# New orders for groups 1 to 8 of a linear-attention and GELU kernel: three seven-product units in group 2

## The chip, the cores and the metric

The kernel runs on one core of one Trainium2 chip. The metric is the device time of one execution in microseconds (us); the kernel before is given by the median of three runs. One execution was also taken with the hardware profiler.

## The reference

Inputs q, k and v have the shape (8 batches, 8 heads, 576 positions, 64 wide); the weights are `w_in` (512 x 2048) and `w_out` (2048 x 512). For each batch and head:

```
phi(x) = where(x > 0, x, exp(x) - 1) + 1
kv  = phi(k).T @ v                  # 64 x 64
z   = sum of phi(k) over positions  # 64
x   = (phi(q) @ kv) / (phi(q) @ z + 1e-6)
h   = x @ w_in                      # the 8 heads side by side: 512 wide
out = gelu_tanh(h) @ w_out          # 4608 x 512, float32
```

## The kernel before

The work is cut into nine groups, j = 0 to 8. Groups 0 to 7 take the first 512 positions of one batch each; group 8 takes the last 64 positions of all eight batches together. While TensorE (PE in the profile) makes the two large products of group j, the attention of group j + 1 is put between them.

Both large products are made by a scheme of seven products with sums instead of eight products without (Strassen in Winograd's form). For `h`, class `Quad` (L997) takes a unit of 512 columns of `h`, called X, Y, Z or W by its place. One unit is seven products of four matmuls with 256 columns each (L1007), and between them VectorE (DVE) and ScalarE (ACT) copy and add on the accumulator banks. Where there is no unit, a block of 128 columns is made plainly: word `p`, four matmuls with 512 columns (L365), followed by one GELU, word `g`. A unit stands in place of four `p`. The seven products of the second matmul, words `o1` to `o7`, have 16 matmuls with 256 columns each (L812).

The order of all instructions on all engines is written out, one string for each group, `ORDER_A` (group 0) to `ORDER_I` (group 8). `iteration` (L1073) goes through the words of a string, and each engine executes its own instructions in the order of the words. So a word that waits holds up everything behind it on its engine. The words that matter here, with `U` for one of X, Y, Z, W:

| word | what it issues | line |
|---|---|---|
| `U1` ... `U7` | one product of a unit, 4 matmuls | L1007 |
| `Us` | copies `U1` into the seed bank, where `U2` then adds (ACT; DVE with a ') | L1041 |
| `Um`, `Uu` | copies of a bank into SBUF (m: DVE, ACT with a '; u: ACT, DVE with a ') | L1046, L1050 |
| `Uc`, `Ua` | additions on DVE | L1035 |
| `Ug11` ... `Ug22` | the four GELUs of a unit on ACT | L1022 |
| `S1:a-b` ... `S4:a-b` | sums of the GELU results for blocks a to b, on DVE: `S3` before `o7`, `S2` before `o6` | L772 |
| `os`, `oc11`, `oc12`, `oc21`, `oc22`, `om`, `ou` | copies and additions after the `o` products | L902 to L933 |
| `!xs` | four differences of the next group's x on DVE, used by products 7, 6, 5, 4 | L995 |
| `n0` ... `n3` | attention of one chunk: 4 matmuls, then a division on DVE | L287, L304, L305 |
| `k` | phi(k).T @ v, 72 small matmuls, then two DVE copies | L271, L630 |
| `t0`, `t1`, `!qta`, `!qtb`, `!rt` | transposes of x and of phi(q) on TensorE, then a copy (ACT; DVE with a ') | L664, L644, L654 |
| `!ke`, `!qe`, `!re` | exp on ACT | L240 |
| `!kx`, `!qx`, `!rx`, `!km`, `!qm`, `!rm` | the other parts of phi on DVE | L248, L256 |
| `!vc` | cast of v (ACT; DVE with a ') | L260 |
| `!lk`, `!lq`, `!lv`, `!lr` | loads from the SP queue into a pool of seven buffers | L90, L99, L113 |
| `!t` | loads the table of GELU on ACT | L398 |
| `@1` | stores of the group before, issued by ACT | L946 |

There are six single accumulator banks and one pair. The seed bank goes from unit to unit: `Us` of the next unit writes it after `Ug11` of the unit before has read it. exp and GELU are in different tables. Where ACT comes to a function whose table is not there and no `!t` stands ahead, the compiler writes a table load just ahead of that function, behind those waits of it that are written as instructions of their own.

Two of the seven load buffers hold sums for good, and from group 2 on a third holds rows of the units (word `!br`). A load gets the buffer that comes free first, and SP issues its loads in the order of the words.

Of the kernel before, what the change touches and what calls it, by code (L numbers as in the profile page):

```python
# [17 lines left out]
def kernel(  # L18
# [293 lines left out]
    xs = {}  # L312
# [760 lines left out]
    def iteration(j):  # L1073
# [65 lines left out]
        "o0:12-16 @32 o1:12-16 @33 !qe:2 o2:12-16 @34 o3:12-16 @35"  # L1139
    )  # L1140
    ORDER_B = (
        "!qx:2 !qm:2 p8 !ke:2 p5 !t p1 p0 !qtb:2' !kx:2 g0 p2 g1 g2 !vc:2' p3 g3 !km:2 !lk:3 p11 "
        "p4 g4 g5 !a0 p7 p6 g6 !a2 g7 !a3 k2 !lv:3 !qta:2 o1 os' g8 @2 p9 p12 p10 !qx:3 g9 n0 "
        "T0-8 !lk:4 p14 g10 g11 g12 p13 n1 g13 !lq:4 g14 !kxb:3 p15 g15 o7 S1:2-3 S1:1-2 S1:0-1 "
        "!ke:3 o2 S1:3-8 S2:0-8 om !qe:3 n2' !vc:3 t0 n3 o6 !kxa:3 ou' o4 o5 !qm:3 !qtb:3 S4:0-8 "
        "oc22 oc21 t1 !km:3 !qta:3' o3 oc12' !xs oc11'"
    )
    ORDER_C = (
        "k3 p0 p14 Z1 !lv:5 !ke:4 !kx:4 !t p6 Z7 !br Zs g6 @1 Z6 Zu Zm n1 Z2 !qx:4 Zg11 g14 p8 Z5 "
        "Y1 !km:4 Zc g0 g8 Ys Y7 p7 Z4 n2 Y6 Ym' !lv:4 g7 !lk:5 Y2 Yg11 Z3 Zg12 Zg22 p15 Y4 Yu' "  # L1150
        "Za Ya Y5 Yc p1 Zg21 g15 g1 n3' n0 Yg22 Y3 Yg12 o1 Yg21 p9 S1:3-8 S3:4-8 os g9 t1' t0 "
        "S1:0-3 o2 !qe:4 S3:0-4 S2:0-8 o7 om !xs S4:0-8 o6 ou' !qm:4 o4 !vc:4 o5 !kx:5 !ke:5 oc22 "
        "oc11 oc21 !qta:4' k4 o3 oc12' !km:5"
    )
    ORDER_D = (
        "X1 Y1 !lq:5 !t Xs !qtb:4' X2 Xg11 Ys X6 Xu' n0 X7 Z1 Y2 !lk:6 Xm' Yg11 X5 Zs Xc Xg22 Y7 "
        "Ym n1 Y6 Yu' X3 Xg12 Z2 @1 X4 Xa Zg11 W1 Ws Xg21 Y4 Ya Yg21 Y5 Yc Z6 Zu' W6 Wu' Yg22 Z7 "
        "Zm' W2 Y3 Wg11 W7 Wm' Yg12 Z5 !vc:5' W5 Zc Z4 Zg22 Za W4 Wc Wa Z3 Zg12 S1:0-6 Wg22 Zg21 "
        "o1 os W3 Wg12 Wg21 S2:0-6 t0 S1:6-8 k5 S2:6-8 S3:0-8 !qx:5 n2' S4:0-8 o2 !ke:6 o6 !kx:6 "
        "!lv:6 ou o7 om !qe:5 n3 o5 oc11 o4 !vc:6 !qm:5 oc22 oc21 t1' !qta:5' !qtb:5 !xs o3 oc12"  # L1160
    )
    ORDER_E = (
        "X1 Xs !t X7 n2 Xm Y1 X6 !lq:6 X2 Xu' Xg11 n1 Y7 X4 Ys Z1 Ym' Y2 @1 X5 !km:6 Xc Yg11 Zs "
        "Y6 Y4 Xa Yu Ya !lr:0 k6 Xg22 Xg21 Z6 Zu' X3 Yg21 Z2 Zg11 !rx:0 W1 Ws Y5 Yc n3 Z7 Z5 Zm' "
        "Zc W6 Z4 Xg12 Yg22 !lv:7 Y3 Yg12 W7 Zg22 W2 Wg11 Wu' W5 Z3 Zg12 Wm Wc Wg22 W4 Za n0 W3 "
        "Wa Wg12 S1:0-8 !lk:7 S2:0-8 Zg21 o1 os Wg21 t1 t0 o2 !re:0 o6 S3:0-8 o7 ou oc11 !vc:7' "
        "om !qe:6 S4:0-8 !kx:7 o5 !xs !ke:7 oc22 !qx:6 !re:1 o4 oc21 o3 oc12"
    )
    ORDER_F = (
        "!t !qm:6 X1 Xs' X7 Xm' Y7 Ym !qta:6' X2 Xg11 X6 Y4 Xu' Y1 !km:7 Ys X4 !qtb:6 X5 Xa Xg21 "  # L1170
        "Y2 Xc Xg22 Y6 Yu' Z1 Ya k7 Yg11 Y5 Yc X3 Zs Z7 Xg12 Z2 Zg11 Zm n1 W1 Ws Y3 Z6 W6 @1 "
        "!lq:7 !qx:7 Wu' Yg21 W2 Z4 Zu Z5 Zc Yg12 Yg22 S1:0-4 W7 Wm' n0 Wg11 W5 Z3 Zg12 Wc Zg22 "
        "o1 W3 Wg22 !rm:0 Wg12 t0 S1:4-6 S3:0-6 W4 S1:6-8 S3:6-8 !lr:1 S2:0-4 S2:4-8 n2 o7 os "
        "!rx:1 !qe:7 om' !rm:1 o6 ou' Wa Wg21 n3 Za Zg21 o4 o5 t1 o2 !qm:7 oc22 S4:0-8 oc21 oc11' "
        "!qtb:7 !xs o3 oc12'"
    )
    ORDER_G = (
        "X1 !qta:7' Xs X7 Y7 Ym' @1 X2 Xg11 Xm n2 X6 Y1 !rt:0' Ys Y4 n0 Xu Y6 Y2 !rx:2 Z1 X4 Yu "
        "Yg11 Ya Zs X5 Y5 Z2 Z6 Yg21 Xa Xg21 Xc Zu' Zg11 W1 Yc n3 Z7 Ws X3 Xg12 W6 Wu' Xg22 Zm "
        "Yg22 Z5 Y3 W7 Wm' W2 Zc W5 Wc Z4 Yg12 W4 Za Zg22 Wa Wg11 n1 Z3 Zg12 S1:0-6 W3 Wg12 Zg21 "  # L1180
        "Wg22 Wg21 !re:3 o1 os' S1:6-8 S2:0-8 t1' S3:5-8 !rt:1 t0 S3:0-5 S4:0-8 o2 o6 ou o7 oc11 "
        "o5 !re:2 !xs !rm:2 om o4 !rx:3 oc22 o3 oc21 oc12' !t"
    )
    ORDER_H = (
        "X1 Xs n1' n0 X7 Xm' X6 X2 Xu Y1 !rt:2' X5 Xg11 Y7 Z1 Xc Ys Y6 @1 Y2 Yu' Ym' Y4 Ya X4 X3 "
        "Xa Y5 Xg22 Yg11 Zs Z6 Yc Xg12 Yg21 Zu' Z2 Zg11 Xg21 Z7 W1 Y3 Z5 Ws' W7 Yg22 Yg12 W6 Wu "
        "Zm W2 Wg11 Z4 W5 Wm Zc Zg22 !rm:3 Wc Wg22 Z3 Zg12 !rt:3' W4 Wa W3 Wg12 Za Zg21 o1 os "
        "S1:6-8 S1:0-6 S2:0-8 S3:0-8 n3' n2 Wg21 t0' o2 o6 o7 ou o5 om oc22 t1 o4 S4:0-8 oc11 !xs "
        "o3 oc21 oc12'"
    )  # L1190
    ORDER_I = (
        "X1 Xs Y1 X7 X2 Xg11 Xm @1 X6 Ys Xu' X4 Y7 Ym' X5 Y2 Yg11 Z1 Y6 Xa Xg21 Xc Zs' Yu' Y4 Ya "
        "X3 Z6 Z2 W1 Xg22 Xg12 Zg11 Z7 Y5 Zu' Z5 Ws W6 Yg21 Zm W2 Yc Yg22 Wg11 Wu' W7 Y3 Yg12 W5 "
        "Zc Z3 Wm Zg12 Wc Zg22 Z4 Za Wg22 W4 S1:0-6 W3 Wg12 S1:6-8 S2:0-3 S2:3-8 Wa o1 Wg21 "
        "S3:0-8 Zg21 S4:3-8 S4:0-3 o5 o6 o7 o2 o4 o3"
    )
    ORDERS = {0: ORDER_A, 1: ORDER_B, 2: ORDER_C, 3: ORDER_D, 4: ORDER_E, 5: ORDER_F, 6: ORDER_G, 7: ORDER_H, 8: ORDER_I}

# [33 lines left out]
```

## Time and profile before

| | us |
|---|---|
| three runs | 275.84, 276.32 (median), 276.67 |
| the profiled execution | 276.67 |
| its span, first to last instruction | 274.9 |
| around the span | 1.77 |

The profile has one row for a kind of instruction, with busy time, mean duration and the idle time ahead of it. A timeline has one row for consecutive instructions of one kind: start, time taken, engine, line, result and operands, count; the idle time ahead and what ended it stand in square brackets. PEld is the weight load that goes with each matmul and overlaps it; DVE is VectorE, ACT ScalarE, POOL GpSimd. The time recorded for a row of matmuls is some 0.16 us longer than their pitch, because they are pipelined: a product of four takes 0.60 us in its row, and the next begins 0.44 us after its start.

The groups begin at about 48.5 (group 1), 79.5 (2), 108.5 (3), 137 (4), 164 (5), 192.5 (6), 219.8 (7) and 246.7 us (8).

### The profile page before, as it was taken

The numbers are of one execution on the slowest core, as the hardware profiler recorded it, in microseconds if no ns is written. First come the engines' busy times: TensorE is split into PE (matmuls) and PEld (weight loads), VectorE is DVE, ScalarE is ACT, GpSimd is POOL, SyncE is SP. The second block draws the span as 40 slices with busy tenths as digits, with TensorE's granted clock in tenths as the row PEclk, the third lists the DMA queues.
The fourth block names the chain that finished last, engine by engine and source line by source line (L and its number), as shares of the span: only waits on it lengthen the run. The fifth ranks groups of instructions, "written<-read, shape, count | busy, mean of one in ns | idle before, by whom it ended". The sixth has DMA issues, their size and how long they took to land.

```text
span 274.9 us, 7015 instructions
## 1 busy us (share of the span) xinstructions
PE 267.9 (97%) x2988; PEld 215.2 (78%) x2989; DVE 241.1 (88%) x394; ACT 204.7 (74%) x290; POOL 18.4 (7%) x30
## 2 busy tenths in 40 slices
PE   8899999999999999999999999999999999999995
PEld 3484446466977799988989988989999889888884
DVE  2979996898999998999999999999899689967982
ACT  4758876957987797888898898886688388338820
POOL 7057401000000000000000000000000000000000
PEclk9999999999999999999999999999999999999999
DMA  6999999996197019731493055101200030003004
GB/s 229 401 405 397 410 405 401 400 403 244 39 364 238 31 25 346 283 104 55 89 342 147 2 161 148 79 1 41 114 2 0 17 141 0 2 2 154 0 2 153
DMA packets 29327, 46.58 MB, mean 169 GB/s; under 512 B 5232, under 2 KB 15472, under 8 KB 29296
## 3 DMA queue, kind: packets, MB, share of 16 engines
q1 hardware_dynamic: 26416, 37.23, 38.2%
q10 hardware_dynamic: 2880, 8.91, 8.0%
q8 instruction: 23, 0.38, 0.6%
q14 instruction: 8, 0.07, 0.1%
HBM read 36.70 MB, written 9.44 MB: 168 GB/s over the span
## 4 chain that ended last, share of the span: by engine, by line
PE 82%; DVE 6%; DMA 5%; ACT 2%; SPq 2%; POOL 1%; issue 1%
PE o_ps L812 31%; PE hq_ps L1007 25%; PE h_ps L365 6%; DMA w_st<-in_moe_w_in_dram 5%; PE h_ps L812 4%; PE h_ps L1007 4%; PE n_ps L287 2%; PE t_ps L664 2%; PE o_ps L739 2%; PE t_ps L644 2%; PE kv_ps L271 2%; DVE w_B L977 2%; DVE w_near L977 2%; DVE w_A L977 1%; SPq L90 1%; ACT k_e L240 1%
## 5 line engine op out<-in xcount | busy, mean ns | idle before, releaser
L812 PEld LDWEIGHTS <-g 128*128 128x128 f16 x624 | 60.3, 98 | 7.0
L812 PE MATMUL o_ps<-w_out_sb,g 128*128 128x256 f16 x384 | 45.7, 273 | 0.0
L365 PE MATMUL h_ps<-xt,w_in_sb 128*128 128x512 f16 (+2 forms) x212 | 37.8, 327 | 0.2 <-ACT g L385 0.2
L1022 ACT ACTIVATE g<-hq_ps 128x512 f16<-128x512 f32 x52 | 31.1, 620 | 3.4 <-PE hq_ps L1007 1.3
L1007 PEld LDWEIGHTS <-w_in_sb 128*128 128x128 f16 x312 | 30.2, 98 | 4.1
L365 PEld LDWEIGHTS <-w_in_sb 128*128 128x128 f16 x212 | 17.9, 98 | 14.6 <-issue 0.5
L812 PEld LDWEIGHTS <-s 128*128 128x128 f16 x272 | 26.5, 98 | 3.2
L385 ACT ACTIVATE g<-h_ps 128x512 f16<-128x512 f32 x40 | 22.3, 602 | 7.5 <-PE h_ps L365 7.3
L305 DVE TENSOR_TENSOR xs<-n_ps,r 128x512 f16<-128x512 f32 (+1 forms) x42 | 25.3, 603 | 1.4
L1007 PE MATMUL hq_ps<-t_sum,w_near 128*128 128x256 f16 x168 | 24.2, 272 | 0.0
L1007 PEld LDWEIGHTS <-w_near 128*128 128x128 f16 x224 | 21.4, 98 | 2.9
L933 DVE TENSOR_TENSOR o_sb<-o_ps,o_sb 128x512 f32<-128x512 f32 (+1 forms) x21 | 13.0, 636 | 7.6 <-PE o_ps L812 3.9
L1022 ACT ACTIVATE g<-h_ps 128x512 f16<-128x512 f32 x26 | 16.1, 619 | 4.6 <-PE h_ps L1007 4.3
L1035 DVE TENSOR_TENSOR rows<-hq_ps,rows 128x512 f32<-128x512 f32 x26 | 17.8, 686 | 1.0 <-PE hq_ps L1007 0.2
L240 ACT ACTIVATE q_e<-q_x 128x2048 bf16<-128x2048 f32 (+1 forms) x9 | 15.5, 1722 | 3.3 <-DMA q_x<-in_q_dram 3.2
L1035 DVE TENSOR_TENSOR hq_ps<-hq_ps,rows 128x512 f32<-128x512 f32 x26 | 17.5, 693 | 0.5 <-PE hq_ps L1007 0.2
L240 ACT ACTIVATE k_e<-k_x 128x2304 bf16<-128x2304 f32 (+1 forms) x9 | 17.2, 1910 | 0.8 <-DMA k_x<-in_k_dram 0.7
L1022 ACT ACTIVATE g<-rows 128x512 f16<-128x512 f32 x26 | 16.7, 652 | 1.2 <-DVE rows L1035 1.2
L1041 ACT COPY h_ps<-hq_ps 128x512 f32<-128x512 f32 x23 | 13.1, 571 | 5.9 <-PE hq_ps L1007 5.4
L1007 PE MATMUL h_ps<-xt,w_in_sb 128*128 128x256 f16 x104 | 15.6, 272 | 0.0
L812 PE MATMUL o_ps<-w_B,g 128*128 128x256 f16 x128 | 15.3, 273 | 0.0
L812 PE MATMUL o_ps<-w_near,s 128*128 128x256 f16 x128 | 15.3, 273 | 0.0
(129 smaller groups left out, 512.5 us busy)
## 6 DMA issues: line engine op xcount, KB each, us to landing
out_dram<-o_sb ACTq DMA_DIRECT2D x16, 512.0 KB, 3.0
k_x<-in_k_dram SPq DMA_DIRECT2D x7, 1152.0 KB, 10.6
v_x<-in_v_dram SPq DMA_DIRECT2D x7, 1152.0 KB, 9.0
q_x<-in_q_dram SPq DMA_DIRECT2D x6, 1024.0 KB, 7.8
w_st<-in_moe_w_in_dram SPq DMA_DIRECT2D x3, 1024.0 KB, 13.5
q_x<-in_q_dram SPq DMA_DIRECT2D x4, 512.0 KB, 8.9
w_st<-in_moe_w_out_dram SPq DMA_DIRECT2D x2, 1024.0 KB, 10.7
w_st<-in_moe_w_out_dram SPq DMA_DIRECT2D x4, 512.0 KB, 9.1
```

What stands on the lines that cost most here:

```text
L240: nc.scalar.activation(o, i, AF.Exp)
L271: nc.tensor.matmul(kv_of(a, ii)[HP * s : HP * (s + 1)], lhsT=kp[r, j, u, :], rhs=vp[r, j, u, :], start=(j == 0), stop=(j == J - 1), skip_g ...
L305: nc.vector.tensor_tensor(x_v, n_v[heads + (slice(0, D),)], r[heads + (None,)].to_broadcast(shape + [D]), op=ALU.mult,)
L365: nc.tensor.matmul(h_ps[:, ts], lhsT=w_in_sb[:, c, P * m : P * (m + 1)], rhs=xt[:, c, ts], start=(c == 0), stop=(c == KM - 1), skip_group_ ...
L385: nc.scalar.activation(g_v, h_v, AF.Gelu_apprx_tanh)
L812: nc.tensor.matmul(ps[t] if type(ps) is list else ps[:, t, :], lhsT=lhs[:, m, P * t : P * (t + 1)], rhs=rhs[:, m, :], start=(first and m = ...
L933: nc.vector.tensor_tensor(out, i0, i1, op=ALU.add)
L977: nc.vector.tensor_tensor(out, i0, i1, op=op)
L1007: nc.tensor.matmul(ps[:, f], lhsT=lhs[:, c, P * f : P * (f + 1)], rhs=rhs[:, c], start=(first and f == 0 and c == 0), stop=(c == KM // 2 - 1),
L1022: nc.scalar.activation(g_v, src, AF.Gelu_apprx_tanh)
L1035: add = lambda out, i0, i1: nc.vector.tensor_tensor(out, i0, i1, op=ALU.add)
L1041: on(nc.scalar.copy, nc.vector.tensor_copy)(self.seed, self.b)
```

## The change

Only the strings `ORDER_B` to `ORDER_I` are changed. In group 2 the plain blocks `p0`, `p1`, `p8`, `p9` with their four GELUs are replaced by the unit X, so that the group has three units and four plain blocks instead of two and eight. All groups from 1 on are put in a new order: copies move between ACT and DVE (the mark '), sums are cut at other places, and some steps go to another group. Among them: `!ke:4` from group 2 to group 1, `!km:5` and the first transposes of q of batch 4 from 2 to 3, the loads `!lv:5` from 2 to 3, `!lq:6` from 4 to 3, `!lq:7` from 5 to 4 and `!lr:0` from 4 to 2, `!rx:0` from 4 to 3. In group 5 `!qe:7` goes behind the last GELUs; group 6 has its `!t` at the end, as before. Group 0 and the functions stay as they are.

Cut to groups 2, 3 and 6 and one place of 5:

```diff
     ORDER_B = (
...
     ORDER_C = (
-        "k3 p0 p14 Z1 !lv:5 !ke:4 !kx:4 !t p6 Z7 !br Zs g6 @1 Z6 Zu Zm n1 Z2 !qx:4 Zg11 g14 p8 Z5 "
-        "Y1 !km:4 Zc g0 g8 Ys Y7 p7 Z4 n2 Y6 Ym' !lv:4 g7 !lk:5 Y2 Yg11 Z3 Zg12 Zg22 p15 Y4 Yu' "
-        "Za Ya Y5 Yc p1 Zg21 g15 g1 n3' n0 Yg22 Y3 Yg12 o1 Yg21 p9 S1:3-8 S3:4-8 os g9 t1' t0 "
-        "S1:0-3 o2 !qe:4 S3:0-4 S2:0-8 o7 om !xs S4:0-8 o6 ou' !qm:4 o4 !vc:4 o5 !kx:5 !ke:5 oc22 "
-        "oc11 oc21 !qta:4' k4 o3 oc12' !km:5"
+        "Z1 @1 !br Z7 !t p14 p6 Zs' Z2 g6 Zg11 !kx:4 Zm Y1 Z6 p7 g14 !lv:4 !lr:0 Z4 Ys g7 Y7 Y6 "
+        "!km:4 Y2 Ym' Zu' Z5 Yu Za Zg21 Y4 Yg11 p15 Zc Z3 !qx:4 Ya X1 g15 Xs' Zg22 Zg12 k3 Y5 Yc "
+        "Yg21 X6 X7 Xu n1 X2 Xm' Xg11 Yg22 X5 Xc Xg22 n2' X4 Xa n3 Y3 Yg12 X3 Xg12 S1:0-8 S2:0-8 "
+        "Xg21 o1 os !vc:4 t1 n0 !qe:4 o2 S3:0-8 S4:0-8 o6 ou' !lk:5 k4 !kx:5 t0 !xs o7 o5 om o4 "
+        "!ke:5 oc22 oc11 oc21 o3 !qm:4 oc12'"
     )
     ORDER_D = (
-        "X1 Y1 !lq:5 !t Xs !qtb:4' X2 Xg11 Ys X6 Xu' n0 X7 Z1 Y2 !lk:6 Xm' Yg11 X5 Zs Xc Xg22 Y7 "
-        "Ym n1 Y6 Yu' X3 Xg12 Z2 @1 X4 Xa Zg11 W1 Ws Xg21 Y4 Ya Yg21 Y5 Yc Z6 Zu' W6 Wu' Yg22 Z7 "
-        "Zm' W2 Y3 Wg11 W7 Wm' Yg12 Z5 !vc:5' W5 Zc Z4 Zg22 Za W4 Wc Wa Z3 Zg12 S1:0-6 Wg22 Zg21 "
-        "o1 os W3 Wg12 Wg21 S2:0-6 t0 S1:6-8 k5 S2:6-8 S3:0-8 !qx:5 n2' S4:0-8 o2 !ke:6 o6 !kx:6 "
-        "!lv:6 ou o7 om !qe:5 n3 o5 oc11 o4 !vc:6 !qm:5 oc22 oc21 t1' !qta:5' !qtb:5 !xs o3 oc12"
+        "!t !lv:5 X1 !rx:0 !vc:5' !lq:5 Xs !qta:4' Y7 Ym' Y1 X2 Xg11 Y4 X7 !km:5 X6 !qtb:4' Ys Y6 "
+        "Xu X5 Xm' Yu Y2 Yg11 Xc Xg22 Z1 Ya Yg21 Zs' n1 X4 X3 Y5 Yc Xg12 Z2 W1 Zg11 !lv:6 Ws Xa "
+        "Z6 Zu' Y3 Z7 W6 Yg12 Z5 Zm Wu' Zc W7 W2 Yg22 Xg21 Wm' W5 Wc n0 Z3 Zg22 Z4 Wg11 W3 W4 "
+        "Wg22 o1 S1:0-4 S3:0-4 @1 Zg12 Wa Wg12 S1:4-8 Wg21 S3:4-8 Za S2:0-6 S2:6-8 os k5 !vc:6 "
+        "n2' o7 om Zg21 !lk:6 !qe:5 o6 S4:0-8 t0 !lq:6 ou' n3 o2 oc11 o5 t1 !qx:5 !qm:5 oc22 "
+        "!ke:6 !xs o4 o3 oc21 oc12 !kx:6"
     )
...
     ORDER_F = (
...
-        "!lq:7 !qx:7 Wu' Yg21 W2 Z4 Zu Z5 Zc Yg12 Yg22 S1:0-4 W7 Wm' n0 Wg11 W5 Z3 Zg12 Wc Zg22 "
-        "!rx:1 !qe:7 om' !rm:1 o6 ou' Wa Wg21 n3 Za Zg21 o4 o5 t1 o2 !qm:7 oc22 S4:0-8 oc21 oc11' "
+        "Zg22 Wg12 t0 S1:4-6 S1:6-8 S3:4-8 Z4 S2:0-8 Wg21 n3 Za o7 os !qx:7 !rx:1 !rm:1 n2' om "
+        "Zg21 o6 o4 !rm:0 ou o5 S4:0-8 !qe:7 oc22 t1' o2 oc21 o3 oc11 !qm:7 !xs oc12 !qtb:7'"
...
     ORDER_G = (
-        "X1 !qta:7' Xs X7 Y7 Ym' @1 X2 Xg11 Xm n2 X6 Y1 !rt:0' Ys Y4 n0 Xu Y6 Y2 !rx:2 Z1 X4 Yu "
-        "Yg11 Ya Zs X5 Y5 Z2 Z6 Yg21 Xa Xg21 Xc Zu' Zg11 W1 Yc n3 Z7 Ws X3 Xg12 W6 Wu' Xg22 Zm "
-        "Yg22 Z5 Y3 W7 Wm' W2 Zc W5 Wc Z4 Yg12 W4 Za Zg22 Wa Wg11 n1 Z3 Zg12 S1:0-6 W3 Wg12 Zg21 "
-        "Wg22 Wg21 !re:3 o1 os' S1:6-8 S2:0-8 t1' S3:5-8 !rt:1 t0 S3:0-5 S4:0-8 o2 o6 ou o7 oc11 "
-        "o5 !re:2 !xs !rm:2 om o4 !rx:3 oc22 o3 oc21 oc12' !t"
+        "X1 !qta:7' X7 !rt:0' Xs Xm X2 X6 Y1 Xu' n0 Y7 Xg11 X4 Ys Ym Y2 Xa Z1 n2 Yg11 Zs Y6 Yu @1 "
+        "X5 Xg21 Xc Y4 Z2 Zg11 Ya Yg21 Z6 W1 Ws' Zu' X3 Y5 Yc Xg22 n1 W6 Xg12 Wu Z7 Zm Yg22 Z5 W2 "
+        "Wg11 W7 Wm' Zc W5 Wc Z4 Zg22 Y3 Z3 W4 Za Wa Yg12 n3 Zg12 W3 Wg12 Wg22 Zg21 o1 !rx:2 os "
+        "S1:0-8 S2:0-8 !rt:1' S3:0-8 Wg21 !re:3 t0' t1 o2 o6 ou o7 !rx:3 S4:0-8 oc11' !re:2 om' "
+        "!xs o5 oc22 o4 !t oc21 o3 !rm:3 !rt:3' oc12"
     )
...
```

## The prediction

> **What bounds the kernel now.** I read the page first: span, busy times, and the slices.
>
> ```profile
> span 274.9 us, 7015 instructions
> PE 267.9 (97%) x2988; PEld 215.2 (78%) x2989; DVE 241.1 (88%) x394; ACT 204.7 (74%) x290; POOL 18.4 (7%) x30
> PE   8899999999999999999999999999999999999995
> ```
>
> PE is full in every slice but the first two and the last. Next, what PE waited for from 48.5 us on, where the changed groups begin. The answer has one line:
>
> ```profile
> PE h_ps L365 <- ACT g L385: 0.2, 1, 0.2
> ```
>
> Such a list leaves out short waits, so I also took the starts of successive matmuls against their usual pitch. From 48.5 us to the end of the products that finds 0.36 us in group 1 at 53.1, 0.29 us in group 8 around 248 to 252, 0.10 us at 220.9, and the 0.21 us of switching at each `k`. So PE's own work is the time, and a new order can gain at most that work taken away plus some 0.75 us of waits. The third view, busy time by group (us, then PE, PEld, DVE, ACT, POOL; the rows are groups 2, 3, 4, 5 and 6), says how much the helpers have left:
>
> ```profile
> 79.50:108.50 29.00, 29.00 (x385) 23.11 (x385) 27.47 (x47) 24.63 (x31) 0.00 (x0) 1.00 0.51 173
> 108.50:137.00 28.50, 28.50 (x355) 25.80 (x354) 27.69 (x44) 24.27 (x34) 0.00 (x0) 1.00 0.45 140
> 137.00:164.00 27.00, 27.00 (x330) 24.22 (x328) 26.22 (x42) 24.59 (x36) 0.00 (x0) 1.00 0.48 166
> 164.00:192.00 28.00, 28.00 (x350) 25.15 (x349) 27.20 (x47) 22.46 (x32) 0.00 (x0) 1.00 0.19 62
> 192.00:219.50 27.50, 27.50 (x278) 24.94 (x276) 23.57 (x43) 18.94 (x34) 0.00 (x0) 1.00 0.09 36
> ```
>
> DVE is busy for 95 to 97% of groups 2 to 5 and yet never late: the old order fits to a tenth of a microsecond. The granted clock is 1.00 throughout (the column before the DMA share).
>
> **The change part by part.**
>
> **1. The unit X in group 2.** The chain of waits gives both prices: a plain block, and 28 matmuls with 256 columns.
>
> ```profile
> 89.93 0.86 PE h_ps L365 x4
> ...
> 114.83 3.06 PE hq_ps L1007 x28
> ```
>
> Four blocks are 16 matmuls at 216 ns (the pitch), 3.46 us; the unit is 28 at 109 ns, 3.05 us. PE gains 0.40 us. On ACT four GELUs go and four come, and `Xu`, `Xm'` are new (0.48 us each in a row of copies). On DVE `Xs'`, `Xc`, `Xa` are new (0.60 us each in a row, 0.69 alone), 1.8 us. Who pays for them? In the same group `Zs'` and `Zu'` come to DVE, while `Yu`, the copy of `t1` and that of `!qta:4` leave it, and `!km:5` (1.27 us) goes to group 3: about even. Summed so for every word, with one price for each kind, DVE's work changes by -1.2, -0.2, +1.1, +2.4, -2.4, +1.8, +0.3 and -0.1 us in groups 1 to 8. Up to the end of group 5 the sum is level, and the 1.7 us that are left over fall where DVE has 3 to 6 us free. As a sum, DVE does not become the bound; only its order can cost (4, and the second rival). The cover for these words is PE's 28 us in each group; without it they would cost their 1.8 us.
>
> A rule speaks against this part. The Trainium skill, "Perfetto Trace Analysis", section Identifying the Most-Contended Engine, judges TensorE's headroom by the busy time of weight loads, not of matmuls; that is 78% here. Were the loads the bound, the unit's 12 more at 98 ns would cost 1.2 us where I take off 0.40. The trace shows the matmuls one behind the other at their pitch, so I go by the matmuls.
>
> **2. The table load at the start of group 6.** In group 5 `!qe:7` now comes after the last GELU, and there is no `!t` before `Xg11` of group 6. So the load of GELU's table moves there. The trace of before has one such load, in group 5, and what stands around it matters:
>
> ```profile
> 186.09 1.28 ACT L1022 ACT_TABLE_LOAD   x1 [0.92 <-DVE hq_ps L1035]
> 187.38 1.08 ACT L1022 ACTIVATE g<-hq_ps 128x512 f16<-128x512 f32 x2
> ```
>
> ACT stood idle for 0.92 us until DVE had made the input of the GELU, and only then loaded the table: such a load sits behind the wait of its GELU, not ahead of it. Nothing on PE was near it then. In group 6 PE is: `Xg11` waits for `X2`, `Ys` behind it on ACT needs the seed bank that `Xg11` reads, and `Y2` needs `Ys`. These rows give the steps (PE to copy, copy, GELU to copy):
>
> ```profile
> 192.51 0.60 PE L1007 MATMUL hq_ps<-xt,w_in_sb 128*128 128x256 f16 x4
> 193.14 0.57 ACT L1041 COPY h_ps<-hq_ps 128x512 f32<-128x512 f32 x1 [0.81 <-PE hq_ps L1007]
> ...
> 195.00 0.60 ACT L1022 ACTIVATE g<-h_ps 128x512 f16<-128x512 f32 x1
> ```
>
> From the start of `X2`: its end 0.60, to ACT 0.03, load 1.28, step 0.01, GELU 0.60, step 0.03, copy 0.57, to PE 0.06: `Y2` can start at 3.18 us. By PE's own pitch it would start after `X2`, `X6`, `Y1`, `Y7`, `X4` (0.437 each) and `n0` (0.236): 2.42 us. PE waits 0.76 us. Queued behind it is all of PE; on ACT, `Ys` and all after it. The other end of this cost is nothing, if the load should run ahead of the wait while ACT is idle after `Xs`. I take 0.76, by the row of the one load of this kind. Group 5 keeps its exp table load and loses this one, which held nothing up.
>
> The Trainium skill, "ScalarE: Activation LUTs", section What ACT_TABLE_LOAD costs, adds a drain of about 1.38 us to the load and puts a switch at 2.66 us. By that, an estimate, PE would wait 2.1 us here and the kernel would take 278.4. In the rows above the GELU begins 0.01 us after the load, with no drain between, so I keep 1.28.
>
> **3. `o1` to `o2` in group 2.** `o2` adds to the seed bank that `os` fills with `o1`. Group 4 of before shows the shortest such passage (the matmuls end 0.16 us after the next row's start):
>
> ```profile
> 152.67 1.06 PE L664 MATMUL t_ps<-ident_x,xs 128*128 128x128 f16 x16
> 152.93 0.57 ACT L902 COPY h_ps<-o_ps 128x512 f32<-128x512 f32 x1 [0.72 <-PE o_ps L812]
> ...
> 153.56 0.49 PE L812 MATMUL h_ps<-w_out_sb,g 128*128 128x256 f16 x3
> ```
>
> From the end of `o1` in PE's order (152.67) to `o2` it is 0.89 us, with `o2` starting 0.06 us after the copy ends: all of it needed, and filled there by 16 transposes. The new group 2 has only `t1` (0.445) and `n0` (0.236) between: 0.68. PE waits 0.21 us; at the other end nothing, if `t1` itself is held by the division of `n3` and so fills the gap. I take 0.21.
>
> **4. Sums at the turn from `h` to `out`.** In the new group 3, with 0 at the start of `o1`, `o7` starts at 2.78 (`o1` 1.75, `k` 0.80, `n2` 0.24) and `o6` at 4.53. DVE has `Wc` and the division of `n0` done at -0.3 (`W5` ends at -2.0), then `S1:0-4`, `S3:0-4`, `Wa`, `S1:4-8` at 0.60 each, `S3:4-8` at 0.69: 2.79, just enough. Then `Za` 0.60 and the two pieces of `S2`, 0.87 and 0.42: 4.6, with the step to PE 0.15 too late. I take 0.15; the ends are nothing and 0.4, should DVE enter this stretch late by a copy or two. In group 1, `S1` must wait for `o7` to have read the tile that it writes, and the same count gives `S2` 0.1 to 0.2 after `o6` could start. Against it stand the 0.36 us that group 1 waited at 53.1, which the new order of blocks may shorten; I set both against each other, at nothing, with ends of -0.5 and +0.3.
>
> **5. All else moved.** The number of transposes, attention pieces, exps and explicit table loads is the same over the kernel, so PE's sum changes by part 1 alone. `n0'` instead of `n2'` and the like only exchange one pair of banks for two. Stores at `@1` follow the last copy of the group before on ACT, as they did. The SP queue has the same loads in a new order: `!lr:0` now ahead of `!lk:5`, and `!lv:5` behind it. What hides a load is that its buffer comes free 10 us or more ahead of the use; the tightest is batch 5's v, the third rival. POOL has no work after 45 us. Groups 4, 5, 7 and 8 go at nothing, covered by the same 28 us of PE; their ends are -0.3 (the waits in group 8) and +0.3 each.
>
> **The sum.** -0.40 + 0.76 + 0.21 + 0.15 = +0.72 us. The profiled execution took 276.67 us, a span of 274.9 and 1.77 around it; it would become 277.4. It stands 0.35 above the median of 276.32, so for the median I predict 277.0, or 0.26% more: just inside the 0.3% (0.83 us) that a measurement of this kernel can tell from no change.
>
> **The rivals.**
>
> *The load runs early, the order fits.* ACT loads the table after `Xs` while it waits, or the wait is covered. Then -0.40 + 0.36 at most is left, or -0.7 with group 1's wait gone: 275.6 to 276.3, say 276.0. For it: the old order had no such slips. Against: the row at 186.09.
>
> *DVE is late at every turn.* Place: `S1` to `S3` in groups 1 to 5, where DVE is busy for 95% and more. Price: if it reaches each turn 0.2 to 0.3 us late, +1.0 to +1.5 on top of the sum less its own 0.15, so 278.1 (277.4 to 279). It decides the verdict from 0.1 us in all. For it: group 4's DVE work grows by 2.4 us. Against: level sums to the end of group 5.
>
> *Batch 5's v lands late.* The cast `!vc:5'` is DVE's second step in group 3, and the load can only be issued when a buffer is free. If that is batch 4's v, cast 2.7 us after the end of `o1` in group 2, there are 10.7 us until `!vc:5'`.
>
> ```profile
> v_x<-in_v_dram SPq DMA_DIRECT2D x7, 1152.0 KB, 9.0
> ```
>
> 9.0 us fit. If the buffer is that of batch 5's k, free only 1.8 us before group 3, DVE stands for 6 us, and everything behind it; PE goes on for some 2 us until copies and banks are missing: +4, so 281.
>
> **How the numbers follow.** My forecast, 277.0 (276.6 to 277.5), has 0.46; the early load 0.18; DVE at every turn 0.27; the late v 0.05; a new order that also clears all old waits, under 275.5, 0.04. Of the forecast four tenths lie above 277.15, so slower has 0.18 + 0.27 + 0.05 = 0.50, the same 0.28 + 0.18 = 0.46, faster 0.04. The range goes from 275.8 (inside the early load's case) to 278.8 (inside DVE's); about 2 in 10 is left out.
>
> **What would show it.** Part 1: in group 2, 28 more matmuls at L1007 and 16 fewer at L365. Part 2: early in group 6 a table load at L1022 with idle time ahead of it that `X2` ended, and a hole of some 0.76 us in PE before a product into h_ps. Part 3: 0.2 us between `n0` and `o2` in group 2. Part 4: waits of PEld at L812 for DVE at L772. Wrong would be a load in group 6 right behind `Xs`, or PE waiting in group 3 for banks behind the cast at L260.

## The result, and the profile after

The changed kernel takes 277.85 us in the median of four runs (277.71 to 278.00), the kernel before 276.40 beside it on the same chip: 1.0055 times as long, with an interval of 1.0038 to 1.0072. That is 1.45 us more, where 0.7 was forecast. The profiled execution took 277.71 us. From the page of the changed kernel:

```profile
span 275.9 us, 7052 instructions
PE 268.9 (97%) x3000; PEld 216.4 (78%) x3001; DVE 242.4 (88%) x394; ACT 203.4 (74%) x292; POOL 18.9 (7%) x30
PE   8999999999999999999999999999999999999995
```

In slices of 7 us nothing is to be seen: PE looks as full as before. The waits of PE, from 45 us on, show one line more than before:

```profile
PE h_ps L1007 <- ACT h_ps L1041: 0.6, 1, 0.6
PE h_ps L365 <- ACT g L385: 0.2, 1, 0.2
```

The third view is again the busy time by group (us, then PE, PEld, DVE, ACT, POOL), groups 2 to 6 of the changed kernel:

```profile
78.93:107.43 28.50, 28.47 (x390) 23.79 (x388) 26.95 (x44) 24.75 (x34) 0.00 (x0) 1.00 0.54 171
107.43:135.75 28.32, 28.26 (x346) 25.03 (x344) 27.23 (x47) 24.52 (x34) 0.00 (x0) 1.00 0.54 182
135.75:164.18 28.43, 28.32 (x347) 25.12 (x345) 27.34 (x44) 23.78 (x36) 0.00 (x0) 1.00 0.31 107
164.18:192.16 27.98, 27.98 (x346) 25.18 (x344) 26.96 (x46) 21.09 (x33) 0.00 (x0) 1.00 0.29 97
192.16:220.59 28.43, 27.79 (x283) 25.09 (x280) 25.30 (x45) 19.57 (x31) 0.00 (x0) 1.00 0.06 25
```

PE's busy time falls short of the group's length by 0.64 us in group 6 and by up to 0.11 in others. The recorded time of a product overhangs its pitch by 0.16 us, so shorter waits stay hidden in this view. I therefore set the starts of successive matmuls against their pitch, as in the prediction, for both traces. From the first matmul of group 1 to the end of the last matmul it is 222.91 us before (48.53 to 271.44) and 224.37 after (48.10 to 272.47): 1.46 more, as the medians say. The two profiled times lie only 1.04 apart because group 0, which is the same in both, ended 0.43 earlier in the second. The 1.46 us come from these places:

| place (time after) | before | after | what ended the wait | forecast |
|---|---|---|---|---|
| group 2: unit X for four blocks | | -0.40 | 28 x 109 ns for 16 x 216 ns | -0.40 |
| group 2: `o2` (95.4) | 0 | 0.19 | seed copy `os`, ACT | 0.21 |
| group 3: `W2` to `W5` (118.5) | 0 | 0.22 | copy `Wu'`, DVE | 0 |
| group 3: `o6` (125.7) | 0 | 0.06 | sums `S2`, DVE | 0.15 |
| group 4: `X2` (137.4) | 0 | 0.27 | seed copy `Xs`, ACT | 0 |
| group 4: `n0` (148.8) | 0 | 0.16 | division of `n3`, DVE | 0 |
| group 6: `Y2` (196.5) | 0 | 0.81 | seed copy `Ys`, ACT, behind a table load | 0.76 |
| group 7: one more switch to small matmuls | | 0.22 | | 0 |
| group 7: 220.9, gone | 0.10 | 0 | | 0 |
| group 1: 53.1, 52.7 after | 0.36 | 0.36 | a GELU, ACT | 0 |

Together +1.43; the rest is below 0.05 us at any one place. Group 6 in the timeline of the changed kernel:

```profile
194.15 0.60 PE L1007 MATMUL h_ps<-xt,w_in_sb 128*128 128x256 f16 x4
...
194.83 1.28 ACT L1022 ACT_TABLE_LOAD   x1 [0.96 <-PE h_ps L1007]
...
196.13 0.60 ACT L1022 ACTIVATE g<-h_ps 128x512 f16<-128x512 f32 x1
...
196.76 0.57 ACT L1041 COPY h_ps<-hq_ps 128x512 f32<-128x512 f32 x1
...
197.38 0.60 PE L1007 MATMUL h_ps<-xt,w_in_sb 128*128 128x256 f16 x4 [0.64 <-ACT h_ps L1041]
```

ACT stands for 0.96 us until `X2` (194.15) has ended, and only then loads the table. `Y2` starts 3.23 us after `X2`; the prediction had 3.18. The turn from `h` to `out` in group 2:

```profile
94.82 0.61 PE L664 MATMUL t_ps<-ident_x,xs 128*128 128x128 f16 x8
95.07 0.57 ACT L902 COPY h_ps<-o_ps 128x512 f32<-128x512 f32 x1 [0.48 <-PE o_ps L812]
95.27 0.40 PE L287 MATMUL n_ps<-kvbd,qt 128*128 128x130 bf16 x4
95.56 2.15 ACT L260 CAST vp<-v_x 128x2304 bf16<-128x2304 f32 x1
95.69 1.03 PE L812 MATMUL h_ps<-w_out_sb,g 128*128 128x256 f16 x8
```

The seed copy ends at 95.64 and `o2` starts at 95.69, 0.87 us after the end of `o1` in PE's order (94.82); `t1` and `n0` fill 0.68 of it.

And two of the places that no step of the prediction named, first group 3, then the start of group 4, in the same view:

```profile
117.49 0.69 DVE L1046 COPY rows<-hq_ps 128x512 f32<-128x512 f32 x1 [0.24 <-PE hq_ps L1007]
...
118.10 0.68 DVE L1050 COPY rows<-hq_ps 128x512 f32<-128x512 f32 x1
...
118.83 0.60 PE L1007 MATMUL hq_ps<-t_sum,w_A 128*128 128x256 f16 x4
...
135.98 0.34 ACTq L946 DMA_DIRECT2D out_dram<-o_sb  x1
136.20 0.60 PE L1007 MATMUL hq_ps<-xt,w_in_sb 128*128 128x256 f16 x4
136.36 0.59 ACT L929 COPY o_sb<-o_ps 128x512 f32<-128x512 f32 x1 [0.86 <-PE t_ps L644]
...
137.17 0.57 ACT L1041 COPY h_ps<-hq_ps 128x512 f32<-128x512 f32 x1 [0.23 <-ACT o_sb L929]
...
137.79 0.60 PE L1007 MATMUL h_ps<-xt,w_in_sb 128*128 128x256 f16 x4
```

In group 3 `Wu'` empties the bank that `W5` needs, and `W5` starts 0.05 us after it. `Wu'` stands behind `Zm` on DVE, and `Zm` stood still for 0.24 us, although the product that it copies (`Z7`) had ended at 117.02. The profile puts the wait down to a product on PE; the one that ended just before `Zm` started (0.02 us) is the next, `W6`, which `Zm` does not read.

In group 4 `X2` starts 0.05 us after `Xs` ends and 0.27 late. The copy `oc12` of group 3 stands ahead of `Xs` on ACT, as it did before. From the timeline of the kernel before:

```profile
137.20 0.59 ACT L929 COPY o_sb<-o_ps 128x512 f32<-128x512 f32 x1 [0.59 <-PE o_ps L812]
...
137.69 0.59 ACT L1041 COPY h_ps<-hq_ps 128x512 f32<-128x512 f32 x1
...
138.93 0.60 PE L1007 MATMUL h_ps<-xt,w_in_sb 128*128 128x256 f16 x4
```

There `X2` came 0.65 us after the end of `Xs`, because `X7`, `n2`, `Y1` and `X6` (1.55 us) lay between `X1` and `X2`. In the new order only eight transposes and `Y1` do (0.89 us), and the issue of a store comes right ahead of `oc12`. That alone would have cost little: `X1` ended at 136.80 and `oc12` at 136.95, so with the copy's 0.57 and the step to PE `X2` could have come at 137.57, where 137.52 was its turn. But ACT stood for another 0.23 us between `oc12` and `Xs`; the profile names `oc12` itself for it.

So both holes come where the new order leaves a copy almost no time to spare, and a wait of 0.23 to 0.24 us of the copy itself uses it up. What these two copies waited for is not shown. The words around them alone do not decide it: in experiments 4 and 8 the words around `Zm` are the same, and it does not stand.

### The profile page after: what moved, and what is told of

The parts are those of the page before. It is cut to its first block, busy times and chain, and to the rows that moved or that the text cites. A ratio compares the mean times of both kernels' runs of the same rounds, so it can differ in the third digit from the quotient of the medians.

```text
span 275.9 us, 7052 instructions
## 1 busy us (share of the span) xinstructions
PE 268.9 (97%) x3000; PEld 216.4 (78%) x3001; DVE 242.4 (88%) x394; ACT 203.4 (74%) x292; POOL 18.9 (7%) x30
## 4 chain that ended last, share of the span: by engine, by line
PE 81%; DVE 7%; DMA 5%; ACT 3%; SPq 1%; issue 1%; POOL 1%; ACTq 0%
PE o_ps L812 31%; PE hq_ps L1007 25%; PE h_ps L365 5%; DMA w_st<-in_moe_w_in_dram 5%; PE h_ps L812 4%; PE h_ps L1007 4%; PE n_ps L287 2%; PE t_ps L664 2%; PE o_ps L739 2%; PE kv_ps L271 2%; DVE w_B L977 2%; PE t_ps L644 2%; DVE w_near L977 2%; DVE w_A L977 1%; ACT k_e L240 1%
## 5 line engine op out<-in xcount | busy, mean ns | idle before, releaser
L1007 PEld LDWEIGHTS <-w_in_sb 128*128 128x128 f16 x324 | 31.0, 98 | 5.0 <-issue 1.1
L1022 ACT ACTIVATE g<-hq_ps 128x512 f16<-128x512 f32 x54 | 31.7, 619 | 4.3 <-PE hq_ps L1007 2.1
L365 PE MATMUL h_ps<-xt,w_in_sb 128*128 128x512 f16 (+2 forms) x196 | 33.8, 322 | 0.2 <-ACT g L385 0.2
L365 PEld LDWEIGHTS <-w_in_sb 128*128 128x128 f16 x196 | 16.3, 98 | 13.4 <-issue 0.5
L385 ACT ACTIVATE g<-h_ps 128x512 f16<-128x512 f32 x36 | 20.0, 603 | 4.8 <-PE h_ps L365 4.7
L1022 ACT ACTIVATE g<-h_ps 128x512 f16<-128x512 f32 x27 | 16.7, 620 | 4.6 <-PE h_ps L1007 4.4
L1035 DVE TENSOR_TENSOR hq_ps<-hq_ps,rows 128x512 f32<-128x512 f32 x27 | 18.3, 693 | 1.1 <-ACT rows L1050 0.5
L1022 ACT ACTIVATE g<-rows 128x512 f16<-128x512 f32 x27 | 17.3, 649 | 2.7 <-DVE rows L1035 2.6
L1007 PE MATMUL h_ps<-xt,w_in_sb 128*128 128x256 f16 x108 | 16.2, 272 | 0.8 <-ACT h_ps L1041 0.6
L1007 PE MATMUL hq_ps<-xt,w_in_sb 128*128 128x256 f16 x108 | 16.2, 273 | 0.0
L1007 PE MATMUL hq_ps<-w_A,w_in_sb 128*128 128x256 f16 x108 | 16.0, 272 | 0.0
L1041 ACT COPY h_ps<-hq_ps 128x512 f32<-128x512 f32 x19 | 10.9, 572 | 6.3 <-PE hq_ps L1007 5.7
```

Of the source, the lines that this page charges most:

```text
L365: nc.tensor.matmul(h_ps[:, ts], lhsT=w_in_sb[:, c, P * m : P * (m + 1)], rhs=xt[:, c, ts], start=(c == 0), stop=(c == KM - 1), skip_group_ ...
L385: nc.scalar.activation(g_v, h_v, AF.Gelu_apprx_tanh)
L1007: nc.tensor.matmul(ps[:, f], lhsT=lhs[:, c, P * f : P * (f + 1)], rhs=rhs[:, c], start=(first and f == 0 and c == 0), stop=(c == KM // 2 - 1),
L1022: nc.scalar.activation(g_v, src, AF.Gelu_apprx_tanh)
L1035: add = lambda out, i0, i1: nc.vector.tensor_tensor(out, i0, i1, op=ALU.add)
L1041: on(nc.scalar.copy, nc.vector.tensor_copy)(self.seed, self.b)
```

## The experiments

Each kernel was timed in five rounds beside the kernel before, which took 276.29 to 276.35 us in these (277.85 stands for the changed kernel). Words not shown are unchanged.

**1. The table load ahead of the wait** (`a_t6`, changed kernel, group 6).

```diff
-X7 !rt:0' Xs Xm
+X7 !rt:0' Xs !t Xm
```

> The changed kernel with an explicit table load (word !t) behind Xs at the start of group 6. Theory (the load sits behind the wait of Xg11 and lies on PE's path): the hole of 0.81 us ahead of Y2 goes, the load is done while ACT waits for X2; 277.85 - 0.8 = 277.05, ratio to the kernel before about 1.0025. Rival (ACT or DVE has a backlog at the start of group 6 and the load only stands in it): the hole stays at 0.5 us or more, 277.4 to 277.9.

Measured: 277.12 us (276.95 to 277.77), 1.0036 (1.0022 to 1.0050): 0.73 less than the changed kernel. In its timeline the load runs while ACT would stand, and `Y2` (196.64) follows at PE's pitch:

```profile
193.96 1.28 ACT L398 ACT_TABLE_LOAD   x1
...
195.25 0.60 ACT L1022 ACTIVATE g<-h_ps 128x512 f16<-128x512 f32 x1
...
195.88 0.57 ACT L1041 COPY h_ps<-hq_ps 128x512 f32<-128x512 f32 x1
...
196.64 0.60 PE L1007 MATMUL h_ps<-xt,w_in_sb 128*128 128x256 f16 x4
```

All other holes stay where they were. So the load's place is worth half of the loss, and the other half is not the table.

**2. `Y2` moved two products back instead** (`a_y2`, group 6).

```diff
-X4 Ys Ym Y2 Xa Z1 n2
+X4 Ys Ym Xa Z1 n2 Y2
```

> The changed kernel with Y2 put behind Z1 and n2 in group 6; the table load stays behind the wait of Xg11. Theory (a fixed chain of 3.18 us from the start of X2 to Y2 against PE's cover): the cover grows by 0.437 + 0.236 = 0.67 us, the hole shrinks from 0.81 to some 0.1 us, the time by 0.65 to 277.2. Rival (the load delays everything on ACT, so the wait only moves to the next word that needs ACT): a hole of 0.5 us or more appears ahead of a later product of group 6, and 277.6 to 277.9 stays.

Measured: 277.42 us (277.42 to 277.44). The hole before `Y2` shrinks from 0.81 to 0.14, but 0.20 and 0.14 us open behind it, at 199.1 and 200.2: `Z2` now waits for a seed copy that is late in its turn. So half of the 0.67 us that moving the consumer gained came back within 3 us. The holes leave a gain of 0.33, the medians one of 0.43.

**3. The same load forced in another group** (`a_no5`, group 5 without its `!t`).

```diff
-!t !km:7
+!km:7
```

> The changed kernel without the word !t at the start of group 5, so that the load of GELU's table is put ahead of Xg11 there as well. Theory: it sits behind the wait for X2; from the start of X2 3.18 us to the first product after Ys (Y6), where PE has 5 products, 2.19 us: a hole of 1.0 us ahead of Y6, and 278.85. Rival (the load runs while ACT waits): no hole, 277.85.

Measured: 278.81 us (278.80 to 278.83), 0.96 more than the changed kernel. The new load, in the timeline:

```profile
166.69 1.28 ACT L1022 ACT_TABLE_LOAD   x1 [0.23 <-PE h_ps L1007]
...
167.99 0.60 ACT L1022 ACTIVATE g<-h_ps 128x512 f16<-128x512 f32 x1
168.62 0.57 ACT L1041 COPY h_ps<-hq_ps 128x512 f32<-128x512 f32 x1
```

Again the load sits behind the wait of its GELU, and the seed copy behind both holds PE for 1.04 us. The mechanism of part 2 is shown in two groups, and taken away in one.

**4. The unit taken back** (`a_plain`, group 2: four plain blocks with their GELUs at the places of `X1`, `X7`, `X5`, `X3`, and none of the unit's other words).

> The changed kernel with the unit X of group 2 taken back: p0, p1, p8, p9 and their GELUs at places of X1, X7, X5, X3. Theory (the unit saves PE 0.40 us and its sums on DVE are hidden): 0.40 us more of PE's work, 277.85 + 0.40 = 278.25; less up to 0.2 where o2 or o6 of group 2 wait less. Rival (the unit's work on DVE costs as much as it saves on PE): 277.85 or less.

Measured: 278.11 us (278.01 to 278.53): 0.26 more than with the unit. In the trace group 1 to the end takes 224.76 us, 0.39 more. The holes at 118.5 and 137.4 are gone, though the words of groups 3 and 4 are those of the changed kernel: `Zm` and `Xs` follow the copy ahead of them without a stop here. Others have come, 0.28 at 120.5, 0.15 before `o6` (0.06 with the unit) and 0.09 at 91.8, about as much in all. So the unit is worth its 0.40 us on PE; the hole before `o2` (0.19) stays without it and is the order's, not the unit's.

**5. `n0` behind `o2`** (`a_o2`, group 2: one thing less between `o1` and `o2`).

```diff
-t1 n0 !qe:4 o2 S3:0-8
+t1 !qe:4 o2 n0 S3:0-8
```

> The changed kernel with n0 of group 2 put behind o2, so that t1 alone lies between o1 and o2. Theory (from o1's end to o2 it takes 0.88 us whatever lies between): the hole ahead of o2 grows from 0.19 by the 0.24 us of n0 to 0.43, and the time from 277.85 to 278.1. Rival (t1 or the sums set the start of o2): no change, 277.85.

Measured: 278.48 us (278.47 to 278.54). The hole before `o2` is 0.43 us as expected, 0.24 more: the chain through the seed copy is 0.88 us and whatever PE lacks of it is lost. A second hole was not expected: `o3` waits 0.48 us for a bank that DVE empties late. The waits of PE name both:

```profile
PE o_ps L812 <- DVE o_sb L933: 0.3, 1, 0.3
PE h_ps L812 <- ACT h_ps L902: 0.3, 1, 0.3
```

**6. Three holes mended at once** (`a_fix`: `a_t6`, and one word moved for each hole of groups 3 and 4).

```diff
 group 3
-Zm Wu' Zc
+Zm Wu Zc
 group 4
-Y1 X2 X7 Xm
+Y1 X7 X2 Xm
-Z4 n0 Wu Wg11 W4 Yg12 Wa
+Z4 Wu Wg11 W4 Yg12 Wa n0
```

> The explicit table load in group 6 as before, and three more single moves against holes that the profile shows: group 3, Wu on ACT instead of DVE (hole of 0.22 us ahead of W5); group 4, X7 ahead of X2 (0.27 us, X2 waits for Xs) and n0 behind W4 (0.16 us, n0 waits for DVE's division of n3). Theory (each hole is its own late copy or division): 277.12 - 0.22 - 0.27 - 0.16 = 276.5. Rival (ACT and DVE are full in groups 3 and 4, so a hole that is filled opens again further on): 276.9 to 277.1.

Measured: 277.13 us (277.11 to 277.15), just what `a_t6` alone gives. The three holes went and 0.20 at 120.1, 0.15 at 125.7 (0.06 before), 0.35 at 137.6 and 0.20 at 165.9 took their place. At the third, the product that was put ahead of `X2` waits for a bank of its own, which DVE empties with a copy of transposed q:

```profile
137.27 1.28 DVE L647 COPY qt<-t_ps 128x1024 bf16<-128x1024 bf16 x2
...
138.01 0.60 PE L1007 MATMUL hq_ps<-t_sum,w_B 128*128 128x256 f16 x4 [0.18 <-DVE qt L647]
```

**7. Two more mended** (`a_fix2`: `a_fix`, and in group 7 the two small attention pieces side by side, to save one switch, and in group 8 one copy from DVE to ACT).

```diff
 group 7
-Yg21 n2 W1
+Yg21 n3' n2 W1
-Zc n3 Yg12
+Zc Yg12
 group 8
-X3 Yu' Y5
+X3 Yu Y5
```

> As the run before, and in group 7 n3 put next to n2 (one switch of PE into the small matmuls and back less, 0.21 us) and in group 8 Yu on ACT instead of DVE (0.14 us ahead of Y5). Theory: 276.5 - 0.35 = 276.15, level with the kernel before or 0.2 under it. Rival (two banks for n3 are not free in time, or DVE's two divisions hold a copy): 276.4 or more.

Measured: 279.44 us (279.37 to 279.48), 2.3 us worse than `a_fix`. The waits of PE:

```profile
PE hq_ps L1007 <- ACT h_ps L1041: 1.2, 1, 1.2
PE hq_ps L1007 <- DVE xs L305: 1.1, 1, 1.1
```

The switch is saved (0.2 us), but the two pieces take both banks, and the next product waits until DVE has divided the first of them, a hole of 1.25 us at 228.4. In group 8 ACT reaches `Yu` only at the end of a wait of 1.20 us for a product; DVE's next addition needs it, and a seed copy behind it holds PE for 1.37 us.

**8. New orders for groups 1 to 3 alone** (`h1`: groups 4 to 8 as before the change; the loads and transposes that went from one part to the other are put back at the seam).

> Groups 1 to 3 of the changed kernel, groups 4 to 8 of the kernel before; what had been moved over the seam is put back (load of the rest of q and the load of q 6 to group 4, transposes of q 5 to the end of group 3). Theory (the load in group 6 and the holes of groups 4 and 7 belong to those groups' new orders): 277.85 - 0.81 - 0.27 - 0.16 - 0.21 = 276.4, with some tenths more if the seam has a hole of its own. Rival (they come from the unit X, whose DVE work is pushed into the later groups): holes of like size remain in groups 4 to 7, 277.0 or more.

Measured: 277.02 us (276.98 to 277.34), 1.0025 (1.0015 to 1.0036). The holes of groups 4, 6 and 7 are gone. The seam itself costs 0.49 us at 138.0 and 0.10 at 140.9: ACT has `oc12` ahead of `Xs`, as in the changed kernel. Hole for hole, 0.19 in group 2, 0.11 in group 3, 0.59 at the seam and 0.15 in group 8, less the unit's 0.40, give +0.64, and 0.67 was measured. The time is the one that the rival gave, but groups 5 and 6 have no hole and group 7 only the old one at 220.9; what the theory left out is the seam. In group 3 the words around `Zm` are those of the changed kernel; `Zm` does not stand here (117.24, when DVE is free), and the hole before `W5` is 0.05 instead of 0.22.

**9. New orders for groups 1 and 2 alone** (`h2`: unit X, and all from group 3 on as before). In group 2 the load `!lv:5` takes the place of `!lr:0`, and the end of the group leads over to the old group 3:

```diff
-k4 !kx:5 t0 !xs o7 o5 om o4 !ke:5 oc22 oc11 oc21 o3 !qm:4 oc12'
+k4 !kx:5 t0 o7 o5 !qm:4 om o4 !ke:5 oc22 !xs oc11 oc21 !qta:4' o3 oc12' !km:5
```

> Groups 1 and 2 of the changed kernel, so the unit X alone, and groups 3 to 8 of the kernel before; the load of v 5, the minimum of k 5 and the first transposes of q 4 are put back into group 2. Theory (the unit is worth 0.40 us, less 0.19 ahead of o2): 276.3 - 0.40 + 0.19 = 276.1, if the end of group 2, which is filled by hand, has no hole; with a hole of half a microsecond there 276.6. Rival (X overfills DVE in group 2, so that group 3 starts late): 277 or more.

Measured: 276.71 us (276.50 to 277.60), 1.0015 (1.0007 to 1.0023). Two holes against the kernel before, 0.20 before `o2` and 0.42 at the seam. ACT's explicit table load stood there for the store, which waits for `oc21` on DVE, behind the four differences of `!xs`:

```profile
107.77 1.28 ACT L398 ACT_TABLE_LOAD   x1 [1.98 <-DVE o_sb L933]
...
109.07 0.57 ACT L1041 COPY h_ps<-hq_ps 128x512 f32<-128x512 f32 x1
...
109.69 0.60 PE L1007 MATMUL h_ps<-xt,w_in_sb 128*128 128x256 f16 x4 [0.25 <-ACT h_ps L1041]
```

**10. The seam put right** (`h3`: `h2` with `!xs` behind `oc21`).

```diff
-oc22 !xs oc11 oc21 !qta:4'
+oc22 oc11 oc21 !xs !qta:4'
```

> As h2 (groups 1 and 2 new with the unit X, groups 3 to 8 old), with the four differences (!xs) behind oc21 on VectorE. In h2 the last store of the group before, the load of GELU's table and the seed of X2 stood for 1.98 us behind oc21, and X2 came 0.42 us late. Theory: oc21 can then run at 105.95 instead of 106.69, the store and the load come 0.7 us earlier, the hole of 0.42 us goes, and what is left is the unit's -0.40 and the 0.20 us before o2: 276.71 - 0.42 = 276.3, within 0.1 us of the kernel before (276.3). Rival: the differences, and the copy of the transposed q behind them, become late for product 7 or for the second transposes of group 3, and a hole of 0.3 us or more opens there: 276.6 or more.

Measured: 276.34 us (276.07 to 276.43), 1.0006 (0.9997 to 1.0015): no longer to be told from the kernel before. Store and load come 0.8 us earlier and the hole of 0.42 is gone, as the theory says; but the rival is there too, in part. At 111.5 a product waits 0.26 us for the bank that `Xu'` empties on DVE. The trace adds up: -0.40 + 0.20 + 0.26 = +0.06, and from group 1 to the last matmul it is 222.97 us against 222.91.

**11. That copy moved to ACT** (`h4`: `h3`, group 3).

```diff
-X6 Xu' n0 X7 Z1 Y2 !lk:6 Xm' Yg11
+X6 Xu n0 X7 Z1 Y2 !lk:6 Xm Yg11
```

> As h3, with two copies of unit X in group 3 exchanged between the engines: Xu from VectorE to ScalarE, Xm from ScalarE to VectorE. In h3 one product at 111.86 stood 0.26 us for the bank that Xu' frees, which VectorE reached only at 111.12, behind the second half of phi(k) and a copy of transposed q. Theory: VectorE is the late one there by this single copy; ScalarE can do it at 111.0, the hole goes, and 276.34 - 0.26 = 276.1. Rival: VectorE has no slack left at that place, and the lateness moves to its next step (the division of n0, or Xc): 276.3 or more.

Measured: 276.65 us (276.57 to 276.66), 1.0012 (0.9998 to 1.0027). The rival was right about this place. The hole at 111.5 is gone, and one of 0.35 us opens 1.7 us later, where the addition `Xc` on DVE comes late behind `Xm` and the division of `n0`. DVE's rows there follow one another with hardly a gap, and `Xc` (112.86) begins only after `Xm`:

```profile
111.21 0.20 DVE L304 RECIPROCAL r<-n_ps 128x8 f32<-128x8 f32 x1
...
111.44 0.69 DVE L305 TENSOR_TENSOR xs<-n_ps,r 128x512 f16<-128x512 f32 x1
...
112.05 0.68 DVE L1046 COPY rows<-hq_ps 128x512 f32<-128x512 f32 x1
...
112.86 0.69 DVE L1035 TENSOR_TENSOR rows<-hq_ps,rows 128x512 f32<-128x512 f32 x1
```

The exchange of one hole for the other makes 0.09 of the 0.31 us by which this version is longer than `h3`. Two waits of 0.10 and 0.09 us in group 8, whose words are the same, make 0.19; why they came is not shown.

**12. The hole before `o2` filled** (`h5`: `h4`, with `n1` of group 2 between `n0` and `o2`).

```diff
-X7 Xu n1 X2
+X7 Xu X2
-t1 n0 !qe:4 o2
+t1 n0 n1 !qe:4 o2
```

> As h4, with one attention chunk of group 2 (n1) moved from ahead of X2 to the place between n0 and o2. PE then has 0.92 us of work between o1 and o2, more than the 0.89 us that the seed copy takes. Theory: the 0.20 us hole before o2 goes, and the time is that of h4 less 0.2, about 275.9, so that of the unit's 0.40 us all is kept. Rival: with the chunk gone a product of unit X (X2 or X5) or, behind o6, the transposes t0 come too early for VectorE, and the 0.2 us opens there: the time of h4.

Measured: 280.72 us (279.05 to 280.78), and neither theory nor rival holds. The hole before `o2` is gone, but `n1` now waits for the bank of `n0`:

```profile
97.16 0.69 DVE L305 TENSOR_TENSOR xs<-n_ps,r 128x512 f16<-128x512 f32 x1
...
97.91 0.29 PE L287 MATMUL n_ps<-kvbd,qt 128*128 128x130 bf16 x2 [2.42 <-DVE xs L305]
```

The division of `n0` stands behind the sums `S1` and `S2` on DVE, 1.22 us each, and PE waits 2.58 us at 95.3. That accounts for the profiled run, which took 279.05; the other three took 280.7, and where they lost 1.7 us more no trace shows.

None of these versions is faster than the kernel before; `h3` comes level with it.

## Why the prediction was right and wrong

The direction was right and the size half of it: 0.7 us were forecast and 1.45 measured. The forecast's own band, 276.6 to 277.5, does not hold the 277.85. The outer range, 275.8 to 278.8, does, because it was widened for the rivals, and that is luck as far as the mechanism goes: no step of the sum gave the second half. By its own mark of 277.15 the kernel became slower, and the measured change is clear of none (1.0038 to 1.0072), where the one forecast was called just too small to be told from none. By its own steps:

- **Part 1, the unit, -0.40.** Right: -0.40 by the pitches, and 0.39 between the traces with and without it. PEld's busy time grew by 1.2 us and cost nothing here, so the matmuls were the right thing to count. The Trainium skill, "Perfetto Trace Analysis", section Identifying the Most-Contended Engine, judges TensorE's headroom by MFU (the matmul work done as a share of the peak) and by the busy time of weight loads. The second of these, 78% here, does not show that PE is full.
- **Part 2, the table load, +0.76.** Right in mechanism and place, 0.81 measured; the GELU begins 0.02 us after the load ends. The drain that the Trainium skill, "ScalarE: Activation LUTs", section What ACT_TABLE_LOAD costs, adds to a load is not seen in these rows; the wait is 0.81 us and not the 2.1 that was estimated from that page. Experiments 1 to 3 show it by taking the load out of the wait and by forcing a second one.
- **Part 3, `o1` to `o2`, +0.21.** Right: 0.19, and 0.43 with one chunk less between.
- **Part 4, sums at the turn, +0.15.** Oversized. In group 3 `o6` waits 0.06 us for `S2`. DVE came to the turn as late as the count said, or later (`S1` began 0.26 us before `o1`, and the last piece of `S2` ended 4.88 us after the start of `o1`, not 4.6). But `o6` began before that piece was done, 0.06 us after the end of the first one, at 4.54; the count had let it wait for both. In group 1 the two parts that were set against each other both came to nothing: the old 0.36 us stayed, and no new wait came.

```profile
124.84 1.28 DVE L772 TENSOR_TENSOR s<-s,g 128x1536 f16<-128x1536 f16 x2
125.84 1.59 PE L812 MATMUL o_ps<-w_A,s 128*128 128x256 f16 x13
```

- **Part 5, "All else moved".** This is the step that failed. It put at nothing what the new order does outside the places of parts 1 to 4, "covered by the same 28 us of PE". That cost 0.22 in group 3, of which part 4 had looked at the turn alone, 0.27 + 0.16 in group 4 and 0.22 - 0.10 in group 7, 0.77 us in all; groups 5 and 8 did cost nothing. Added to the first three parts and the 0.06, that is the 1.4. The end of +0.3 given to each of the groups 4, 5, 7 and 8 would have held group 7's part, but not group 4's 0.43, and the sum took the middle of all. And the cover named was the wrong one: 28 us of PE per group hide work as a sum, while a single copy or division is hidden only by the products between its bank's last write and next use. That cover was 0.89 us long before `X2`, 1.31 before `W5` and 1.75 before `n0`, and the copy or division (0.6 to 0.9 us), what stands ahead of it on its engine and the handovers together took 0.16 to 0.27 more. That the new order left no time to spare at these places is shown; why `Zm` and `Xs` stood for 0.23 to 0.24 us in two of them stays open.

Group 7's part is of another kind. The small attention matmuls on a quarter of the array are preceded by 0.09 us and followed by 0.12 beyond the pitch, and the new order has two clusters of them where the old had one. The prediction saw these switches (the 0.21 us at each `k`) and did not count that their number changes.

The rivals: the early load fell (the load did wait). Batch 5's v did not come late: its load, as argued, could go when batch 4's v was cast, at 97.71, and was issued at 97.73. DVE late at every turn gives nearly the measured time, 278.1, but by another mechanism: the sums at the turns cost 0.06 us, and of the three places inside the units two wait for DVE (`W5`, `n0`) and one for ACT (`X2`). What the rival had right is that an order with DVE at 95 to 96% loses tenths at many places; in experiments 6, 10 and 11 most of the holes that were closed reopened within a few microseconds at another copy.

So the expected gain of the unit went into handovers. Even in the version that adds nothing but the unit and the new groups 1 and 2, 0.46 us of waits stand against 0.40 of saved products. Whether a more thorough reordering of groups 1 to 3 would keep some of the 0.40 stays open; three attempts at single places did not.

## What to carry to other kernels

When one engine is full and the order of the others is written by hand, a new order is not costed by sums of work per stage but by handovers: for each product, which copy frees its bank or makes its input, which words stand ahead of that copy on its engine, and how many tenths are left. Give unexamined reorderings a cost rather than nothing, above all where the old order shows no holes; here it was 0.77 us over the five groups 3, 4, 5, 7 and 8, or 0.15 each. And where the function table changes, an explicit load placed where its engine is idle takes the load out of the wait; here one word was worth 0.7 us.

## What the runs showed that was not expected

- Mending did not add up here. Three edits that each removed a hole of 0.16 to 0.27 us gave nothing together (277.13 against 277.12), and two more that were to save 0.35 cost 2.3.
- The price of one more chunk between two products was 2.58 us of PE where 0.2 were to be gained, since its bank was freed behind 2.44 us of sums. Such a wait is long because of what is queued ahead, and not because of the work awaited (0.9 us).
- A cluster of small matmuls on 64 x 64 of the array costs PE 0.09 us on the way in and 0.12 on the way out, the same in the traces before and after, whatever its length (72 matmuls, 32 or 16).
- The same words can wait or not. `Zm` in group 3 stood for 0.24 us in the changed kernel and not at all in experiments 4 and 8, where the words around it are the same. A hole that is found in one order need not be there in the next.
